# Loads and DMA transposes in strict turns in a fused retention and MLP kernel

## Chip, cores, metric

One core of a Trainium2 chip runs the kernel. The metric is the device time of one execution in microseconds. The profile adds one traced execution: busy times, waits, and the granted clock of the tensor engine. Engines are called PE (matmuls; PEld is its weight load), DVE, ACT, POOL and SP (which only issues DMA here).

## The reference

```python
# q, k, v: (B=4, H=8, S=768, D=64) f32
for t in range(S):                     # retention, per head h, gamma_h = 1 - 2**(-5-h)
    state = gamma * state + outer(k[t], v[t])
    y[t] = q[t] @ state / sqrt(D)
x = y in (B*S, H*D) order              # (3072, 512)
h = x @ w_in                           # (512, 2048)
out = (h * cos(h)) @ w_out             # (2048, 512)
```

## The kernel before

Retention runs in chunks of 128 steps. A "pair" is one chunk of two batch elements; there are 12 pairs, and two pairs make a group of 512 tokens for the MLP. For each pair: load q, k, v; scale q (`conv_q`) and v (`conv_v`) on POOL and cast k (`conv_k`) on ACT, all to bf16; transpose q and k into `qkt`; then on PE `stage_a` (k times q), on DVE its mask (`stage_m`), and on PE `stage_y` (output `xt`, and the state). The MLP's two matmuls (`unit_f`, `unit_o`) fill PE between these. Each engine takes its instructions in the order written.

```python
PRE = 5                                              # slots of load buffers
SLOT = [0, 1, 2, 3, 2, 4, 0, 1, 3, 2, 4, 0]          # pair -> slot
def load(eng, p, names):                             # 256 KB each: one tensor, one batch element
    ...
def conv_k(p, on_act): ...                           # ACT: two casts, one for each batch element
def stage_t(p, b): ...                               # 8 PE transposes and a DVE copy (pairs 0 to 3)
def stage_t_dma(p):                                  # pairs 4 to 11
    for b in range(2):
        nc.sync.dma_start_transpose(out=qkt[n][:, b]..., in_=qk[n][:, b]...)
# ... group 0, pairs 0 to 2 ...
conv_k(3, True); conv_q(3, nc.gpsimd)
load(nc.sync, 4, ("q0", "q1")); load(nc.gpsimd, 4, ("k0", "k1", "v0", "v1"))
conv_v(3, nc.gpsimd)
load(nc.sync, 5, ("q0", "q1", "v0")); load(nc.gpsimd, 5, ("k0", "k1", "v1"))
# ...
stage_t(3, 0); stage_t(3, 1)
# ...
conv_q(4, nc.gpsimd); conv_v(4, nc.gpsimd); conv_k(4, True)
stage_t_dma(4)
load(nc.gpsimd, 6, ("q0", "k0", "q1", "k1", "v0", "v1"))   # two pairs ahead
# ... later: cast and transpose pair p+1, fetch pair p+2 or p+3 ...
```

An output bank of PE (there are seven for all of this) comes free only when ACT and DVE have read it.

Of the kernel before, what the change touches and what calls it, by code (L numbers as in the profile page):

```python
# [10 lines left out]
FP32 = mybir.dt.float32  # L11
BF16 = mybir.dt.bfloat16
# [35 lines left out]
def kernel(  # L48
# [9 lines left out]
    nc = tc.nc  # L58
    B, H, S, D = q.shape
    C = 128  # L60
# [3 lines left out]
    HP = H // 2  # L64
    KIN = DM // 128
    KOUT = DF // 128
    NP = B // 2 * NC
    NG = NP // 2
    PRE = 5
# [11 lines left out]
    def sb(shape, dt, name):  # L81
        return const.tile(shape, dt, name=name)
# [14 lines left out]
    w_out_sb = sb([128, KOUT, DM], BF16, "w_out_sb")  # L97


    qf = [[sb([128, H, D], FP32, f"qf{i}_{b}") for b in range(2)] for i in range(PRE)]  # L100
    kf2 = [sb([128, 2, H, D], FP32, f"kf{i}") for i in range(PRE)]
    kf = [[t[:, b] for b in range(2)] for t in kf2]
    vf = [[sb([128, H, D], FP32, f"vf{i}_{b}") for b in range(2)] for i in range(PRE)]
    ob = [sb([128, DM], FP32, f"ob{i}") for i in range(4)]
    NB = 3
    qk = [sb([128, 2, 2, H, D], BF16, f"qk{i}") for i in range(NB)]
# [11 lines left out]
    gq = sb([128, NC, H], FP32, "gq")  # L118
    gk = sb([128, NC, H], FP32, "gk")
    rel = sb([128, 128], FP32, "rel")  # L120


    SRC = {"q": (qf, q), "k": (kf, k), "v": (vf, v)}
# [3 lines left out]
    def load(eng, p, names):  # L127
        bp, c = divmod(p, NC)
        for n in names:
            t, src = SRC[n[0]]  # L130
            b = int(n[1])
            eng.dma_start(  # L132
                out=t[SLOT[p]][b],
                in_=src[2 * bp + b, :, ds(c * C, C)].rearrange("h t d -> t h d"))

    def load_k(p):
        bp, c = divmod(p, NC)
        nc.gpsimd.dma_start(
            out=kf2[SLOT[p]].rearrange("p b h d -> p (b h) d"),
            in_=k[2 * bp : 2 * bp + 2, :, ds(c * C, C)].rearrange("b h t d -> t (b h) d"))  # L140

    def load_w_in(r):
        nc.gpsimd.dma_start(
# [25 lines left out]
                   allow_small_or_imprecise_dtypes=True)  # L169
    load(nc.gpsimd, 0, ("k1", "q1"))  # L170
    load(nc.gpsimd, 1, ("q1",))
    load_k(1)
    load(nc.gpsimd, 0, ("v0", "v1"))
    nc.vector.memset(zero, 0.0)
    nc.vector.memset(lnsc, math.log(scale))
# [19 lines left out]
    def conv_q(p, eng, bs=(0, 1)):  # L195
        for b in bs:
            eng.tensor_tensor(out=qk[p % NB][:, b, 0], in0=qf[SLOT[p]][b],  # L197
                              in1=bc(gq, p % NC), op=ALU.mult)
            if eng == nc.vector:
                clk.run("dve", 0.69)  # L200

    def conv_v(p, eng, bs=(0, 1)):
        for b in bs:
            eng.tensor_tensor(out=vs[p % NB][:, b], in0=vf[SLOT[p]][b],  # L204
                              in1=bc(gk, p % NC), op=ALU.mult)

    def conv_k(p, on_act):
        for b in range(2):
            if on_act:
                nc.scalar.copy(out=qk[p % NB][:, b, 1], in_=kf[SLOT[p]][b])  # L210
                clk.run("act", 0.6)
            else:
                nc.vector.tensor_copy(out=qk[p % NB][:, b, 1], in_=kf[SLOT[p]][b])
# [12 lines left out]
    def stage_t(p, b, fill=0):  # L226
        n = p % NB
        bank = banks.take()
        tr = bank.bitcast(BF16).rearrange("p (w a t) -> p w a t", w=2, a=HP)
        for w in range(2):  # L230
            for a in range(HP):
                nc.tensor.transpose(tr[:, w, a, :], qk[n][:, b, w, 2 * a : 2 * a + 2, :], ident)  # L232
            if w == 0:
                warm(fill)
        copy_bits(qkt[n][:, b], tr)
        clk.run("pe", 0.45)
        banks.give(bank, clk.run("dve", 0.69, clk.pe + 0.1))

    def stage_t_dma(p):
        n = p % NB  # L240
        for b in range(2):
            nc.sync.dma_start_transpose(
                out=qkt[n][:, b].rearrange("p w a t -> p (w a) t"),
                in_=qk[n][:, b].rearrange("p w h d -> p (w h d)"))
# [7 lines left out]
    def stage_a(p, b):  # L252
        n = p % NB
        bk = [banks.take(), banks.take()]
        ap = [t.rearrange("p (a t) -> p a t", a=HP) for t in bk]
        for a in range(HP):
            for j in range(2):
                po = 64 * j
                nc.tensor.matmul(ap[j][:, a, :], lhsT=kt(n, b, a)[po : po + 64, :],  # L259
                                 rhs=qt(n, b, a)[po : po + 64, :],  # L260
                                 tile_position=(po, 0))
        clk.run("pe", 0.3)
        return b, bk, ap, clk.pe
# [54 lines left out]
    def stage_y(p, copy_st=nc.vector.tensor_copy):  # L318
        for b in range(2):
            half_y(p, b)  # L320
        stage_s(p, copy_st)
# [22 lines left out]
    def pair_f(p, r, parts=(0, 1)):  # L344

        g, hf = divmod(p, 2)
        for f in [4 * r + 2 * i for i in parts]:
            bank = banks.take()
            for e in range(2):
                for i in range(KIN):  # L350
                    nc.tensor.matmul(bank[:, ts(e, 256)], lhsT=w_in_t(i, f + e),  # L351
                                     rhs=xt[g % 2][:, i, ts(hf, 256)],
                                     start=(i == 0 and e == 0), stop=(i == KIN - 1),
                                     skip_group_check=True)
            banks.give(bank, act(bank, gt[g % 2][:, f : f + 2, ts(hf, 256)]))
# [129 lines left out]
    for u in range(12):  # L485
        unit_o(0, u % 4, u // 4)
        if u == 7:
            stage_t(2, 0)
            stage_t(2, 1)
            conv_v(2, nc.vector, (0,))  # L490
        elif u == 9:
            stage_m(2, stage_a(2, 0))
            conv_v(2, nc.vector, (1,))
        elif u == 11:
            stage_m(2, stage_a(2, 1))
    conv_k(3, True)
    conv_q(3, nc.gpsimd)
    load(nc.sync, 4, ("q0", "q1"))
    load(nc.gpsimd, 4, ("k0", "k1", "v0", "v1"))
    conv_v(3, nc.gpsimd)  # L500
    load(nc.sync, 5, ("q0", "q1", "v0"))
    load(nc.gpsimd, 5, ("k0", "k1", "v1"))
    for j in range(4):
        unit_o(0, j, 3)
        if j == 1:
            stage_y(2, nc.scalar.copy)
    pair_f(2, 0)
    stage_t(3, 0)
    stage_t(3, 1)
    pair_f(2, 1)  # L510
    attend(3)
    conv_q(4, nc.gpsimd)
    conv_v(4, nc.gpsimd)
    conv_k(4, True)
    stage_t_dma(4)
    load(nc.gpsimd, 6, ("q0", "k0", "q1", "k1", "v0", "v1"))
    pair_f(2, 2)
    pair_f(2, 3, (0,))
    stage_y(3, nc.scalar.copy)
    pair_f(2, 3, (1,))  # L520
    conv_q(5, nc.gpsimd)
    conv_v(5, nc.gpsimd)
    load(nc.gpsimd, 7, ("q0", "k0", "q1", "k1", "v0", "v1"))
    pair_f(3, 0)
    conv_k(5, True)
    stage_t_dma(5)
    pair_f(3, 1)
    pair_f(3, 2)
    conv_q(6, nc.gpsimd)
    conv_k(6, True)  # L530
    conv_v(6, nc.gpsimd)
    pair_f(3, 3)

    def ahead(p):
        if p < NP:
            conv_q(p, nc.gpsimd)
            conv_k(p, True)
            conv_v(p, nc.gpsimd)

    def fetch(p):  # L540
        load(nc.gpsimd, p, ("q0", "k0", "q1", "k1", "v0", "v1"))

    def later(p):
        stage_y(p)
        n = 8 if p == 4 else p + 3 if p > 5 else NP
        if n < NP:
            fetch(n)

    late = []

    def put_off(when, step):
        late.append((when, step))
# [10 lines left out]
    def o_units(g, a, b):  # L563
        for u in range(a, b):
            unit_o(g, *divmod(u, 4))

    o_units(1, 0, 2)
    attend(4)
    stage_t_dma(6)
    o_units(1, 2, 6)  # L570
    later(4)
    attend(5)
    o_units(1, 6, 10)
    later(5)

    for g in range(2, NG + 1):
        for s in range(16):
            hf, r = divmod(s, 8)
            p = 2 * (g + 1) + hf
            if g == 2 and s % 2 == 0 and s < 12:  # L580
                unit_o(1, *divmod(10 + s // 2, 4))
            if g < NG:
                unit_f(g, s)
            if g > 2:
                if g < NG or s < 12:
                    unit_o(g - 1, *divmod(s, 4))
                elif s == 12:
                    last_o(g - 1, 3)
            while late and late[0][0] <= 16 * g + s:
                late.pop(0)[1]()  # L590
            if p < NP:
                if r == 0:
                    ahead(p + 1)
                elif r == 1:
                    if p + 1 < NP:
                        stage_t_dma(p + 1)
                elif r == 2 and p in (6, 7, 8):
                    todo = [stage_a(p, b) for b in range(2)]
                    stage_m(p, todo[0])
                    put_off(16 * g + s + 1, lambda todo=todo, p=p: stage_m(p, todo[1]))  # L600
                elif r == 6 and p in (6, 7, 11):
                    later(p)
                elif (g, s) == (3, 4):
                    fetch(11)
                if (g, s) in joined:
                    join(joined[g, s], 16 * g + s)


# [28 lines left out]
```

## Time and profile before

| | before |
|---|---|
| time, median (range) | 208.92 us (208.87 to 209.34), 3 runs |
| span of the profiled run | 207.6 us |
| PE busy | 199.5 us (96%) |
| granted clock | 1.0 |
| wait of ACT for k (`kf`) | 9.3 us in 7 waits |
| DMA transpose, issue to landing, min/median/max | 2.7/4.6/13.8 us |

PE is busy nearly all the time and its engine order is the critical chain; the lines are in the prediction. Read a slice line as 40 equal parts of the span, each digit the busy tenths. A wait line reads: engine and line, released by what: us in total, times, longest.

### The profile page before, as it was taken

To read this page: it belongs to the slowest core of one execution; us is meant where nothing else is said; L and a number is where in the kernel's file an instruction comes from. 1 tells how busy PE (TensorE), PEld (TensorE's weight loads), DVE (VectorE), ACT (ScalarE), POOL (GpSimd) and SP (SyncE) were. 2 spreads that over 40 slices of the span, in tenths; PEclk is the share of its full clock that TensorE was granted. 3 is DMA by queue.
4 is the path that set the end of the run, shared out by engine and by line. 5 is a ranking of instruction groups with operands and counts; after the bars stand their busy time and mean duration, and the time that the engine had idled before them with its cause. 6 is when DMAs were issued, how large, how long until landed. Compare 5 with 4: busy or idle time off the path is not lost.

```text
span 207.6 us, 4155 instructions
## 1 busy us (share of the span) xinstructions
PE 199.5 (96%) x1624; PEld 113.5 (55%) x1646; DVE 113.3 (55%) x188; ACT 114.1 (55%) x193; POOL 102.3 (49%) x118
## 2 busy tenths in 40 slices
PE   6889999999999999999999999999999999999993
PEld 1467554558997555546544465544465444444452
DVE  4691984554957454869874466854367244443000
ACT  6767872257996336577753754653554653553120
POOL 8999238399999999999995230000000000000000
PEclk9999999999999999999999999999999999999999
DMA  6999999999999999959799931141101100110222
GB/s 158 351 237 203 215 252 287 336 261 358 258 251 257 264 252 254 255 184 218 242 177 92 252 82 50 55 103 51 51 3 51 51 18 36 51 52 21 80 77 78
DMA packets 36644, 33.83 MB, mean 163 GB/s; under 512 B 26768, under 2 KB 29072, under 8 KB 36624
## 3 DMA queue, kind: packets, MB, share of 16 engines
q0 software_dynamic: 7808, 20.98, 39.4%
q1 hardware_dynamic: 27632, 12.23, 25.4%
q10 hardware_dynamic: 1184, 0.36, 0.7%
q8 instruction: 13, 0.21, 0.4%
q14 instruction: 7, 0.06, 0.1%
HBM read 27.26 MB, written 6.29 MB: 162 GB/s over the span
## 4 chain that ended last, share of the span: by engine, by line
PE 91%; DVE 4%; DMA 2%; issue 1%; DVEq 0%
PE bank L381 38%; PE bank L340 32%; PE bank L351 7%; PE bank L281 3%; PE bank L259 3%; PE bank L286 2%; DMA qf<-in_q_dram 2%; DVE am L268 2%; PE bank L398 2%; PE bank L232 1%; PE st_ps L303 1%; DVE qk L197 1%; DVE qkt L216 1%; PE bank L362 1%; PE bank L369 1%
## 5 line engine op out<-in xcount | busy, mean ns | idle before, releaser
L333 DVE TENSOR_TENSOR gt<-bank,cosb 128x512 bf16<-128x512 f32 x96 | 64.9, 689 | 61.9 <-ACT cosb L329 61.4
L329 ACT ACTIVATE cosb<-bank,halfpi 128x512 bf16<-128x512 f32 x96 | 65.1, 688 | 50.0 <-PE bank L340 44.4
L381 PE MATMUL bank<-w_out_sb,gt 128*128 128x512 bf16 x359 | 88.5, 379 | 0.7 <-issue 0.3
L340 PE MATMUL bank<-xt,w_in 128*128 128x512 bf16 x294 | 74.3, 380 | 0.7 <-issue 0.3
L381 PEld LDWEIGHTS <-gt 128*128 128x128 bf16 x368 | 35.5, 98 | 41.2
L340 PEld LDWEIGHTS <-w_in 128*128 128x128 bf16 x304 | 33.7, 114 | 30.9
L268 DVE TENSOR_TENSOR am<-bank,mask 128x512 bf16<-128x512 f32 x48 | 30.4, 682 | 3.9 <-PE bank L259 3.9
L388 ACT COPY ob<-bank 128x512 f32<-128x512 f32 x23 | 13.4, 586 | 18.4 <-PE bank L381 18.4
L204 POOL TENSOR_TENSOR vs<-vf,gk 128x512 bf16<-128x512 f32 x21 | 21.4, 1045 | 2.9 <-PE st_ps L303 2.9
L132 POOL DMA_DIRECT2D vf<-in_v_dram x23 | 20.3, 885 | 4.8 <-DMA w_out_sb<-in_moe_w_out_dram 4.8
L197 POOL TENSOR_TENSOR qk<-qf,gq 128x512 bf16<-128x512 f32 x18 | 18.5, 1051 | 7.8 <-issue 4.9
L132 POOL DMA_DIRECT2D kf<-in_k_dram x21 | 18.9, 901 | 1.8 <-DMA w_out_sb<-in_moe_w_out_dram 1.6
L210 ACT CAST qk<-kf 128x512 bf16<-128x512 f32 x24 | 13.9, 615 | 9.3 <-DMA kf<-in_k_dram 9.3
L290 ACT CAST xt<-bank 128x512 bf16<-128x512 f32 x24 | 12.9, 589 | 6.7 <-PE bank L286 6.7
L132 POOL DMA_DIRECT2D qf<-in_q_dram x18 | 16.2, 902 | 0.8 <-DMA w_in<-in_moe_w_in_dram 0.8
L351 PE MATMUL bank<-xt,w_in 128*128 128x256 bf16 x128 | 14.7, 273 | 0.0
L351 PEld LDWEIGHTS <-w_in 128*128 128x128 bf16 x128 | 13.8, 114 | 0.4
L286 PE MATMUL bank<-am,vs 128*64 128x128 bf16 x192 | 11.6, 220 | 0.0
L281 PEld LDWEIGHTS <-stb 128*64 128x64 bf16 x160 | 8.7, 109 | 4.3 <-issue 3.8
L281 PE MATMUL bank<-qkt,stb 128*64 128x128 bf16 x160 | 10.7, 222 | 0.3 <-DVE am L268 0.3
L286 PEld LDWEIGHTS <-vs 128*64 128x64 bf16 x192 | 9.9, 110 | 0.5 <-issue 0.4
L315 DVE CAST stb<-st_ps 64x512 bf16<-64x512 f32 x12 | 8.2, 685 | 2.7 <-PE st_ps L303 2.6
(46 smaller groups left out, 86.8 us busy)
## 6 DMA issues: line engine op xcount, KB each, us to landing
vf<-in_v_dram POOLq DMA_DIRECT2D x23, 256.0 KB, 5.8
out_dram<-ob SPq DMA_DIRECT2D x23, 256.0 KB, 2.0
kf<-in_k_dram POOLq DMA_DIRECT2D x21, 256.0 KB, 5.7
qf<-in_q_dram POOLq DMA_DIRECT2D x18, 256.0 KB, 5.3
w_out_sb<-in_moe_w_out_dram POOLq DMA_DIRECT2D x4, 512.0 KB, 12.5
qf<-in_q_dram SPq DMA_DIRECT2D x6, 256.0 KB, 8.1
w_in<-in_moe_w_in_dram POOLq DMA_DIRECT2D x3, 512.0 KB, 8.1
kf<-in_k_dram POOLq DMA_DIRECT2D x1, 512.0 KB, 5.4
```

Source lines behind the costliest of these rows:

```text
L132: eng.dma_start(out=t[SLOT[p]][b], in_=src[2 * bp + b, :, ds(c * C, C)].rearrange("h t d -> t h d"))
L197: eng.tensor_tensor(out=qk[p % NB][:, b, 0], in0=qf[SLOT[p]][b], in1=bc(gq, p % NC), op=ALU.mult)
L204: eng.tensor_tensor(out=vs[p % NB][:, b], in0=vf[SLOT[p]][b], in1=bc(gk, p % NC), op=ALU.mult)
L210: nc.scalar.copy(out=qk[p % NB][:, b, 1], in_=kf[SLOT[p]][b])
L268: nc.vector.tensor_tensor(out=am[p % 2][b][j], in0=ap[j], in1=mask.unsqueeze(1).to_broadcast([128, HP, 128]), op=ALU.mult)
L281: nc.tensor.matmul(yp[ts(j, 64), a, :], lhsT=stb[p % 2][:, b, a, ts(j, 64)], rhs=qt(n, b, a), start=True, stop=False, skip_group_check=True)
L286: nc.tensor.matmul(yp[ts(j, 64), a, :], lhsT=vs[n][:, b, 2 * a + j, :], rhs=am[p % 2][b][j][:, a, :], start=(c == 0), stop=True, skip_grou ...
L329: nc.scalar.activation(out=cb, in_=bank, func=AF.Sin, bias=halfpi)
L333: nc.vector.tensor_tensor(out=out, in0=bank, in1=cb, op=ALU.mult)
L340: nc.tensor.matmul(bank, lhsT=w_in_t(i, f), rhs=xt[g % 2][:, i, :], start=(i == 0), stop=(i == KIN - 1))
L351: nc.tensor.matmul(bank[:, ts(e, 256)], lhsT=w_in_t(i, f + e), rhs=xt[g % 2][:, i, ts(hf, 256)], start=(i == 0 and e == 0), stop=(i == KIN ...
L381: nc.tensor.matmul(bank, lhsT=gt[g % 2][:, f, ts(j, 128)], rhs=w_out_sb[:, f, :], start=(f == 0), stop=(f == KOUT - 1))
```

## The change

The intent, as its description and code tell it: no DMA transpose is to share the DMA engines with loads. From pair 3 on a turn is: cast on POOL, transpose, wait for the transpose, only then load the next pair, with q, k and v in one 512 KB transfer each. POOL is held by a tiny copy (`gate`) that reads the output of the first of a pair's two transposes; the second may still run beside the new loads. Pair 3 moves from PE transposes to DMA transposes, and most k casts move to other places in ACT's order: those of pairs 3, 4 and 8 to 11 earlier, that of pair 6 later.

```diff
-    qf = [[sb([128, H, D], FP32, f"qf{i}_{b}") for b in range(2)] for i in range(PRE)]
...
+    both = {n: [sb([128, 2, H, D], FP32, f"{n}f{i}") for i in range(PRE)] for n in "qkv"}
+    gate = sb([128, 2], BF16, "gate")
+    def load_both(p, names):                       # 512 KB each: both batch elements
...
+    def turn(p):
+        conv_q(p, nc.gpsimd)
+        stage_t_dma(p)
+        conv_v(p, nc.gpsimd)
+        if p + 1 < NP:
+            nc.gpsimd.tensor_copy(out=gate, in_=qkt[p % NB][:, 0, 1, HP - 1, 126:])
+            load_both(p + 1, "kqv")                # one pair ahead
...
-    stage_t(3, 0)
-    stage_t(3, 1)
...
+    k_at = {(2, 0): 7, (2, 6): 8, (2, 12): 9, (3, 4): 10, (3, 12): 11}   # casts, (group, unit)
+    t_at = {(2, 1): 7, (2, 8): 8, (2, 15): 9, (3, 6): 10, (3, 13): 11}   # turns
```

Before, the casts of pairs 7 to 11 stood at (2,0), (2,8), (3,0), (3,8), (4,0).

More of the change, by code (lines that the diff above doesn't have):

```diff
@@ L97 @@
     w_out_sb = sb([128, KOUT, DM], BF16, "w_out_sb")
-    qf = [[sb([128, H, D], FP32, f"qf{i}_{b}") for b in range(2)] for i in range(PRE)]
-    kf2 = [sb([128, 2, H, D], FP32, f"kf{i}") for i in range(PRE)]
-    kf = [[t[:, b] for b in range(2)] for t in kf2]
-    vf = [[sb([128, H, D], FP32, f"vf{i}_{b}") for b in range(2)] for i in range(PRE)]
+    both = {n: [sb([128, 2, H, D], FP32, f"{n}f{i}") for i in range(PRE)] for n in "qkv"}
+    qf, kf, vf = [[[t[:, b] for b in range(2)] for t in both[n]] for n in "qkv"]
     ob = [sb([128, DM], FP32, f"ob{i}") for i in range(4)]
@@ L134, in load @@
                 in_=src[2 * bp + b, :, ds(c * C, C)].rearrange("h t d -> t h d"))
-    def load_k(p):
+    def load_both(p, names):
         bp, c = divmod(p, NC)
-        nc.gpsimd.dma_start(
-            out=kf2[SLOT[p]].rearrange("p b h d -> p (b h) d"),
-            in_=k[2 * bp : 2 * bp + 2, :, ds(c * C, C)].rearrange("b h t d -> t (b h) d"))
+        for n in names:
+            nc.gpsimd.dma_start(
+                out=both[n][SLOT[p]].rearrange("p b h d -> p (b h) d"),
+                in_=SRC[n][1][2 * bp : 2 * bp + 2, :, ds(c * C, C)].rearrange(
+                    "b h t d -> t (b h) d"))
     def load_w_in(r):
@@ L171 @@
     load(nc.gpsimd, 1, ("q1",))
-    load_k(1)
+    load_both(1, "k")
     load(nc.gpsimd, 0, ("v0", "v1"))
@@ L493 @@
             conv_v(2, nc.vector, (1,))
+            conv_k(3, True)
         elif u == 11:
             stage_m(2, stage_a(2, 1))
-    conv_k(3, True)
-    conv_q(3, nc.gpsimd)
-    load(nc.sync, 4, ("q0", "q1"))
-    load(nc.gpsimd, 4, ("k0", "k1", "v0", "v1"))
-    conv_v(3, nc.gpsimd)
-    load(nc.sync, 5, ("q0", "q1", "v0"))
-    load(nc.gpsimd, 5, ("k0", "k1", "v1"))
+    def turn(p):
[5 more added lines that the diff above has]
+            load_both(p + 1, "kqv")
+    turn(3)
     for j in range(4):
@@ L507 @@
     pair_f(2, 0)
-    stage_t(3, 0)
-    stage_t(3, 1)
+    conv_k(4, True)
     pair_f(2, 1)
     attend(3)
-    conv_q(4, nc.gpsimd)
-    conv_v(4, nc.gpsimd)
-    conv_k(4, True)
-    stage_t_dma(4)
-    load(nc.gpsimd, 6, ("q0", "k0", "q1", "k1", "v0", "v1"))
+    turn(4)
     pair_f(2, 2)
@@ L520 @@
     pair_f(2, 3, (1,))
-    conv_q(5, nc.gpsimd)
-    conv_v(5, nc.gpsimd)
-    load(nc.gpsimd, 7, ("q0", "k0", "q1", "k1", "v0", "v1"))
     pair_f(3, 0)
     conv_k(5, True)
-    stage_t_dma(5)
     pair_f(3, 1)
+    turn(5)
     pair_f(3, 2)
-    conv_q(6, nc.gpsimd)
-    conv_k(6, True)
-    conv_v(6, nc.gpsimd)
     pair_f(3, 3)
-    def ahead(p):
-        if p < NP:
-            conv_q(p, nc.gpsimd)
-            conv_k(p, True)
-            conv_v(p, nc.gpsimd)
-    def fetch(p):
-        load(nc.gpsimd, p, ("q0", "k0", "q1", "k1", "v0", "v1"))
-    def later(p):
-        stage_y(p)
-        n = 8 if p == 4 else p + 3 if p > 5 else NP
-        if n < NP:
-            fetch(n)
     late = []
@@ L568 @@
     attend(4)
-    stage_t_dma(6)
-    o_units(1, 2, 6)
-    later(4)
+    o_units(1, 2, 4)
+    conv_k(6, True)
+    o_units(1, 4, 6)
+    turn(6)
+    stage_y(4)
     attend(5)
     o_units(1, 6, 10)
-    later(5)
+    stage_y(5)
+    k_at = {(2, 0): 7, (2, 6): 8, (2, 12): 9, (3, 4): 10, (3, 12): 11}
+    t_at = {(2, 1): 7, (2, 8): 8, (2, 15): 9, (3, 6): 10, (3, 13): 11}
+    a_at = {(2, 2): 6, (2, 10): 7, (3, 2): 8}
+    y_at = {(2, 6): 6, (2, 14): 7, (4, 14): 11}
     for g in range(2, NG + 1):
         for s in range(16):
-            hf, r = divmod(s, 8)
-            p = 2 * (g + 1) + hf
             if g == 2 and s % 2 == 0 and s < 12:
@@ L588 @@
                     last_o(g - 1, 3)
-            while late and late[0][0] <= 16 * g + s:
+            now = 16 * g + s
+            while late and late[0][0] <= now:
                 late.pop(0)[1]()
-            if p < NP:
-                if r == 0:
-                    ahead(p + 1)
-                elif r == 1:
-                    if p + 1 < NP:
-                        stage_t_dma(p + 1)
-                elif r == 2 and p in (6, 7, 8):
-                    todo = [stage_a(p, b) for b in range(2)]
-                    stage_m(p, todo[0])
-                    put_off(16 * g + s + 1, lambda todo=todo, p=p: stage_m(p, todo[1]))
-                elif r == 6 and p in (6, 7, 11):
-                    later(p)
-                elif (g, s) == (3, 4):
-                    fetch(11)
-                if (g, s) in joined:
-                    join(joined[g, s], 16 * g + s)
+            at = (g, s)
+            if at in k_at:
+                conv_k(k_at[at], True)
+            if at in t_at:
+                turn(t_at[at])
+            if at in a_at:
+                p = a_at[at]
+                todo = [stage_a(p, b) for b in range(2)]
+                stage_m(p, todo[0])
+                put_off(now + 1, lambda todo=todo, p=p: stage_m(p, todo[1]))
+            if at in y_at:
+                stage_y(y_at[at])
+            if at in joined:
+                join(joined[at], now)
 _INS = ['q', 'k', 'v', 'moe_w_in', 'moe_w_out']
```

## The prediction

> **What bounds the kernel now.** I read the page first: busy times, slices, chain; then the waits of the tensor engine, the chain in order of time, and the timelines of POOL and ACT. From the page:
>
> ```profile
> PE 199.5 (96%) x1624; PEld 113.5 (55%) x1646; DVE 113.3 (55%) x188; ACT 114.1 (55%) x193; POOL 102.3 (49%) x118
> ...
> PE   6889999999999999999999999999999999999993
> ...
> POOL 8999238399999999999995230000000000000000
> ...
> DMA  6999999999999999959799931141101100110222
> ...
> PE 91%; DVE 4%; DMA 2%; issue 1%; DVEq 0%
> ```
>
> PE is busy in every slice but the first three and the last. POOL is full to about 110 us and then does nothing; DMA is full to about 118 us. So the changed parts (loads, transposes) work in the first 60% of the span and are hidden: PE is what ends late. The waits of PE and the chain in order of time confirm it:
>
> ```profile
> PE bank L415 <- DVE gt L174: 1.2, 1, 1.2
> PE bank L259 <- DVE qkt L216: 1.1, 2, 0.6
> ```
>
> ```profile
> 49.39 0.89 PE bank L232 x16
> ...
> 52.03 0.55 PE bank L259 x16
> ...
> 77.91 1.73 PE bank L340 x8
> ...
> 93.90 3.58 PE bank L340 x16
> 97.47 0.18 PE bank L281 x2
> ...
> 98.91 1.67 PE bank L340 x7
> ```
>
> The longest two waits of PE are at the start (the warm-up and the first transposes). From 16 us to 204 us the chain is PE after PE. Eight matmuls of 512 columns take 1.73 us, 216 ns each, so nothing is to be had by feeding PE better: time falls only if PE work goes, and rises only if something new makes PE wait.
>
> **What the Trainium skill says.** "TensorE: Matmul & The Clock Gate", section "Wait — 56ns, not 53.3ns?", gives 215.7 ns for 512 columns at full clock; the trace agrees (216 ns, granted clock 1.0 in all slices). "DMA: Bandwidth & Descriptors", section "Issuing engines are not separate DMA queues", says that transfers from all issuers share the same 16 DMA engines and interleave; the trace agrees: one transpose took 2.7 us to land when no load ran (136 us) and 13.8 us in the middle of loads (104 us). The same page, section "Anatomy of one DMA — SWDGE (gpsimd) path", puts a POOL transfer at 2.0 us fixed plus bytes over 436 GB/s, 2.6 us for 256 KB; the trace disagrees: 3.8 us at the best in this stretch, issue of 0.88 us included, so I use the trace. The same page, section "Rules for kernel authors", says that a transpose beside ordinary DMAs needs nothing, so the gate is for speed, not for correctness; no run shows it yet.
>
> **The change, part by part.** Removed from PE: the 16 transposes of pair 3 (in the chain above at 49.39), 0.89 us on the path. Their two copies by DVE (681 ns each) were hidden. Pair 3 now takes two DMA transposes, as do pairs 4 to 11 in both kernels. That is all that PE gains: 208.92 - 0.89 = 208.0 us if nothing waits. No other PE work changes in amount; only places of the k casts in ACT's order and of the loads in POOL's.
>
> Loads: 8 pairs times 6 transfers of 256 KB become 8 times 3 of 512 KB. POOL pays 0.88 us for each of the first kind and 1.15 us for the one 512 KB load of before (4.19 us), so 3.45 us in place of 5.3 us a pair. POOL ran the old cycle without a pause, 9.3 us a pair:
>
> ```profile
> 69.49 2.05 POOL L197 TENSOR_TENSOR qk<-qf,gq 128x512 bf16<-128x512 f32 x2
> 71.49 2.04 POOL L204 TENSOR_TENSOR vs<-vf,gk 128x512 bf16<-128x512 f32 x2
> 73.48 0.93 POOL L132 DMA_DIRECT2D qf<-in_q_dram  x1
> 74.40 0.88 POOL L132 DMA_DIRECT2D kf<-in_k_dram  x1
> ```
>
> There a load was issued two pairs ahead, so its landing time was hidden. In the new order POOL does conv_q, conv_v, then the gate (which reads the first transpose's output, so it waits for its landing), then issues the next pair's k, q, v; and the next conv_q needs that q. Now landing is on POOL's cycle. One turn, gate to gate: issue k 1.15; q from issue start to landing, estimated at 4.0 (256 KB loads at 64 to 74 us took 3.8 to 4.7) plus 0.3 longer issue plus 0.3 to 0.8 for twice the data at the 390 GB/s which the busiest moments show: 4.5 to 5.1; conv_q and conv_v 2.05 + 2.04; gate and signals 0.3. The first transpose runs beside conv_v: it starts 1.1 after q, lands 3.1 later (the one at 134.5 us, without loads), q + 4.2, about when conv_v ends, q + 4.1. Sum 10.0 to 10.7, I take 10.3 us. So POOL's work falls, but the cycle grows from 9.3 to about 10.3 us, and no load is ahead of it.
>
> What of it meets PE? The second transpose lands about 1.3 after the gate; k lands about 4.8 after it. Gates: pair 3's inputs land near 40 us as before; the gate of pair 4 cannot come before its k cast, which ACT reaches at 50.2 (behind the two cosines of pair_f(2,0)), so near 54.2. Then 64.5, 74.8, 85.1, 95.4 for pairs 5 to 8. PE's wants, from the chain less 0.89: stage_a of pair 4 at 65.5, 5 at 70.9, 6 at 80.5, 7 at 92.4, 8 at 104, 9 at 119.8, 10 at 128.6. The transposes meet all of them with margin. The k casts don't. They sit in ACT's strict order ahead of work that PE needs:
>
> ```profile
> 91.38 1.12 ACT L210 CAST qk<-kf 128x512 bf16<-128x512 f32 x2
> 92.41 0.69 ACT L329 ACTIVATE cosb<-bank,halfpi 128x512 bf16<-128x512 f32 x1
> ...
> 98.10 1.06 ACT L290 CAST xt<-bank 128x512 bf16<-128x512 f32 x2
> ```
>
> Before, no k cast after 60 us waited for its load. Now the cast of pair 9 is moved ahead from (3,0) to (2,12), where ACT arrives at about 95.5, and its k lands at 95.4 + 4.8 = 100.2. Behind it in ACT stand two cosines (1.3) and the two casts of xt of pair 7 (1.07), after its own 1.12: xt is ready 3.5 after k lands, at 103.7. PE wants it for unit_f(3,0), in the chain inside the piece at 98.91, less 0.89: 98.7. That is a wait of 5.0 us. Pairs 7 (k at 79.3, PE has banks until it lands at 78.6) and 8 (89.6 against some 88.6) cost up to 1 us, inside the 5.0 and not on top, since loads don't wait for PE. Pairs 10 and 11 have 12 and 15 us more of PE work between them and recover. Sum: 208.92 - 0.89 + 5.0 = 213.0 us by this reckoning.
>
> **The rivals.** First, turns are quick enough. With a cycle of 9.4 us pair 9's k lands at about 96 and PE waits 0.7 us at most; the time is 208 to 209. For it: transposes free of loads take 2.7 to 3.1 us, not the median 4.6; whoever placed the casts 8 to 9 us apart reckoned with such a cycle. Against it: conv_q and conv_v alone take 4.1 us and q can hardly land within 5 us of the gate. Second, the cycle is slower: output stores of 256 KB come into some turns, the second transpose overlaps the new loads, 512 KB of short rows is not moved at the best rate. Each 0.5 us in the cycle counts four times at pair 9: with 10.8 us the time is 215. Third, less DMA traffic in PE's way: excluded, since PE runs at 216 ns for a matmul both while DMA is full (77.91, above) and after. Fourth, a wait for pair 3: PE wants its transposes at 51.1, they are issued near 41 to 43, and even 5.6 us (the first transposes under loads) would do. PE's slack here is 3 us; I give it little weight. A gain of over 2% would take 4.2 us of PE time; 0.89 is all there is.
>
> **Range and chances.** The sum says 213.0, the first rival 208.3. The error of the sum is mostly the cycle, plus or minus 0.4 times four and 1 us for ACT's place, and it can only go down to 208.0. I put two thirds on the sum and one third on the rival: 211.5, with 208.0 to 214.8 for 8 in 10. Slower by 2% begins at 213.1: 0.32. Faster by 2%: 0.01. The same: 0.67.
>
> **What would show it.** If right: no piece of L232 near 50 us in the chain, and 16 PE and 2 DVE instructions fewer of that line; POOL no longer full in its slices but with a wait for a qkt transpose and one for q in each turn; transposes landing in about 3 us; ACT waiting for kf between 77 and 101 us, longest for pair 9, some 4 to 5 us; PE idle just before unit_f(3,0), waiting for ACT's cast of xt. POOL's turns end near 125 us instead of 122. If instead ACT waits for kf less than 1 us, the cycle was under 9.5 us and the first rival holds. If PE waits for qkt from a DMA, I was wrong about which product of a turn comes last. If the 216 ns of a matmul change, the third rival was excluded wrongly.

## The result, and the profile after

The changed kernel took 230.69 us, median of 6 runs (228.66 to 231.39); the kernel before 208.89 us in the same rounds. The ratio is 1.102 (95% interval 1.098 to 1.107): slower by 10%. A ratio here and below is the mean time of one kernel's fast runs over the mean of the other's of the same rounds, so not quite the ratio of the medians. Executions over 1.5% slower than the fastest of the same kernel are left out of the means. The profiled run is the quickest of the six: span 225.8 us, granted clock 0.977.

From the page of the changed kernel, busy times, slices and chain:

```profile
PE 203.6 (90%) x1608; PEld 113.8 (50%) x1630; DVE 111.9 (50%) x186; ACT 114.2 (51%) x193; POOL 94.0 (42%) x107
...
PE   7889999999999690999639999999999999999994
...
POOL 8997255856767273947667671500000000000000
PEclk9999999999999998599988999999999999999999
...
PE 68%; DMA 17%; POOL 5%; DVE 4%; issue 3%; ACT 2%; POOLq 0%; ACTq 0%; DVEq 0%
```

PE now has two deep holes (near 87 us and near 113 us), in and after which its clock falls, and a shallow one near 76 us, after which it does not. PE has 16 instructions fewer than before and yet 4 us more of busy time. POOL is no longer full: it waits. The chain, nearly all PE before, now runs through DMA and POOL for over a fifth of the span. The waits say for what:

```profile
POOL qk L198 <- DMA qf<-in_q_dram: 33.7, 9, 5.3
ACT qk L211 <- DMA kf<-in_k_dram: 29.0, 13, 6.6
...
PE bank L341 <- ACT ob L389: 6.5, 1, 6.5
...
PE bank L341 <- ACT xt L291: 5.3, 1, 5.3
...
PE bank L382 <- ACT xt L291: 2.0, 1, 2.0
```

PE waits 13.8 us for ACT, ACT 29 us for k's loads, POOL 34 us for q's. One turn in POOL's timeline (start, us, what; in brackets the idle time before it and who ended it), from the gate of pair 6 to that of pair 7:

```profile
82.72 0.19 POOL L503 COPY gate<-qkt 128x2 bf16<-128x2 bf16 x1 [1.09 <-DMA qkt<-qk]
83.29 1.19 POOL L138 DMA_DIRECT2D kf<-in_k_dram  x1 [0.39 <-issue]
84.48 1.15 POOL L138 DMA_DIRECT2D qf<-in_q_dram  x1
85.62 1.16 POOL L138 DMA_DIRECT2D vf<-in_v_dram  x1
90.29 2.04 POOL L198 TENSOR_TENSOR qk<-qf,gq 128x512 bf16<-128x512 f32 x2 [3.51 <-DMA qf<-in_q_dram]
92.29 2.04 POOL L205 TENSOR_TENSOR vs<-vf,gk 128x512 bf16<-128x512 f32 x2
94.28 0.18 POOL L503 COPY gate<-qkt 128x2 bf16<-128x2 bf16 x1
```

This turn took 11.6 us. The eight gates stand at 44.7, 57.0, 68.3, 82.7, 94.3, 107.6, 118.9 and 130.9 us: 12.3 us a turn in the mean, 11.2 to 14.5. Before, POOL's cycle was 9.3 us. From gate to conv_q, in which POOL issues and then waits for q, it is 7.2 to 7.6 us in six of the eight turns and 9.3 in two. In that stretch the DMA engines stand still first. Windows of half a microsecond behind the gate of pair 5 (the last two figures are DMA share and GB/s):

```profile
68.50:69.00 0.50, 0.50 (x4) 0.23 (x3) 0.50 (x2) 0.00 (x0) 0.20 (x1) 1.00 1.19 209
69.00:69.50 0.50, 0.50 (x4) 0.26 (x3) 0.50 (x2) 0.33 (x1) 0.50 (x1) 1.00 0.00 0
69.50:70.00 0.50, 0.50 (x4) 0.20 (x2) 0.50 (x2) 0.26 (x1) 0.50 (x2) 1.00 0.00 0
70.00:70.50 0.50, 0.50 (x4) 0.20 (x2) 0.45 (x1) 0.00 (x0) 0.50 (x1) 1.00 0.08 8
```

The first load was issued at 68.80; the DMA engines, until then busy with earlier transfers, fall idle at 69.0 and move next to nothing until 70.5 us. On ACT the k casts stand where PE needs ACT:

```profile
88.62 1.14 ACT L211 CAST qk<-kf 128x512 bf16<-128x512 f32 x2 [6.58 <-DMA kf<-in_k_dram]
...
113.16 1.14 ACT L211 CAST qk<-kf 128x512 bf16<-128x512 f32 x2 [5.20 <-DMA kf<-in_k_dram]
114.20 1.26 ACT L330 ACTIVATE cosb<-bank,halfpi 128x512 bf16<-128x512 f32 x2
115.35 1.07 ACT L291 CAST xt<-bank 128x512 bf16<-128x512 f32 x2
```

The first is the cast of pair 7; while ACT waited for its k, PE ran out of banks. The second is pair 9's; behind it stand two cosines and the xt casts that unit_f(3,0) needs. PE's timeline shows its two long waits, and windows of the unit_f matmuls (after the window its length, then PE's busy time in these matmuls, and PEclk as the third figure from the end) show what follows:

```profile
90.87 1.86 PE L341 MATMUL bank<-xt,w_in 128*128 128x512 bf16 x4 [6.46 <-ACT ob L389]
...
116.47 1.86 PE L341 MATMUL bank<-xt,w_in 128*128 128x512 bf16 x4 [5.27 <-ACT xt L291]
```

```profile
90.80:97.10 6.30, 4.61 (x12) 1.48 (x11) 0.59 0.61 140
...
116.40:120.00 3.60, 2.03 (x5) 0.68 (x5) 0.53 0.65 148
```

After each long wait PE ran at a granted clock of 0.59 and 0.53 for 6.3 and 3.6 us. Four matmuls took 1.86 us there against 0.86 us in the rest of the chain.

### The profile page after: what moved, and what is told of

Read it like the earlier page. It is cut to its first block, busy times and chain, and to the rows that moved or that the text cites. A ratio compares the mean times of both kernels' runs of the same rounds, so it can differ in the third digit from the quotient of the medians.

```text
span 225.8 us, 4084 instructions
## 1 busy us (share of the span) xinstructions
PE 203.6 (90%) x1608; PEld 113.8 (50%) x1630; DVE 111.9 (50%) x186; ACT 114.2 (51%) x193; POOL 94.0 (42%) x107
## 4 chain that ended last, share of the span: by engine, by line
PE 68%; DMA 17%; POOL 5%; DVE 4%; issue 3%; ACT 2%; POOLq 0%; ACTq 0%; DVEq 0%
PE bank L382 30%; PE bank L341 28%; DMA qf<-in_q_dram 8%; DMA kf<-in_k_dram 5%; DMA vf<-in_v_dram 3%; DMA qkt<-qk 2%; DVE am L269 2%; PE bank L399 2%; PE bank L260 2%; POOL vs L205 2%; PE bank L282 1%; POOL kf L138 1%; PE bank L287 1%; POOL qk L198 1%; ACT cosb L330 1%
## 5 line engine op out<-in xcount | busy, mean ns | idle before, releaser
L382 PE MATMUL bank<-w_out_sb,gt 128*128 128x512 bf16 x359 | 90.3, 385 | 2.8 <-ACT xt L291 2.0
L341 PE MATMUL bank<-xt,w_in 128*128 128x512 bf16 x294 | 76.9, 390 | 12.4 <-ACT ob L389 6.5
L382 PEld LDWEIGHTS <-gt 128*128 128x128 bf16 x368 | 35.9, 99 | 44.7 <-issue 4.5
L341 PEld LDWEIGHTS <-w_in 128*128 128x128 bf16 x304 | 34.4, 116 | 44.6 <-issue 15.3
L198 POOL TENSOR_TENSOR qk<-qf,gq 128x512 bf16<-128x512 f32 x18 | 18.5, 1045 | 34.1 <-DMA qf<-in_q_dram 33.7
L205 POOL TENSOR_TENSOR vs<-vf,gk 128x512 bf16<-128x512 f32 x21 | 21.9, 1066 | 0.7 <-DMA vf<-in_v_dram 0.7
L352 PEld LDWEIGHTS <-w_in 128*128 128x128 bf16 x128 | 13.8, 114 | 0.7 <-issue 0.3
L138 POOL DMA_DIRECT2D kf<-in_k_dram x9 | 10.7, 1189 | 2.2 <-issue 1.5
L282 PE MATMUL bank<-qkt,stb 128*64 128x128 bf16 x160 | 10.7, 222 | 0.3 <-DVE am L269 0.3
L260 PE MATMUL bank<-qkt 64*128 64x128 bf16 x192 | 8.2, 218 | 1.3 <-DVE qkt L217 1.1
L138 POOL DMA_DIRECT2D vf<-in_v_dram x8 | 9.2, 1152 | 0.0
L138 POOL DMA_DIRECT2D qf<-in_q_dram x8 | 9.2, 1152 | 0.0
## 6 DMA issues: line engine op xcount, KB each, us to landing
w_out_sb<-in_moe_w_out_dram POOLq DMA_DIRECT2D x4, 512.0 KB, 12.3
```

The source lines that it names most:

```text
L138: nc.gpsimd.dma_start(out=both[n][SLOT[p]].rearrange("p b h d -> p (b h) d"), in_=SRC[n][1][2 * bp : 2 * bp + 2, :, ds(c * C, C)].rearrang ...
L198: eng.tensor_tensor(out=qk[p % NB][:, b, 0], in0=qf[SLOT[p]][b], in1=bc(gq, p % NC), op=ALU.mult)
L205: eng.tensor_tensor(out=vs[p % NB][:, b], in0=vf[SLOT[p]][b], in1=bc(gk, p % NC), op=ALU.mult)
L282: nc.tensor.matmul(yp[ts(j, 64), a, :], lhsT=stb[p % 2][:, b, a, ts(j, 64)], rhs=qt(n, b, a), start=True, stop=False, skip_group_check=True)
L341: nc.tensor.matmul(bank, lhsT=w_in_t(i, f), rhs=xt[g % 2][:, i, :], start=(i == 0), stop=(i == KIN - 1))
L352: nc.tensor.matmul(bank[:, ts(e, 256)], lhsT=w_in_t(i, f + e), rhs=xt[g % 2][:, i, ts(hf, 256)], start=(i == 0 and e == 0), stop=(i == KIN ...
```

## The experiments

All kernels gave correct results. "Before" in the same rounds was 208.9 to 209.0 us throughout.

**Loads two pairs ahead, gate kept.**

```diff
+        if p == 3:
+            load_both(4, "kqv")
-        if p + 1 < NP:
+        if p + 2 < NP:
             nc.gpsimd.tensor_copy(out=gate, ...)
-            load_both(p + 1, "kqv")
+            load_both(p + 2, "kqv")
```

> The changed kernel with one thing moved: the loads of a turn are those of the pair after the next (pair 4's loads go out before the first gate); gate, three transfers of 512 KB and the places of the casts stay. Theory (a load that is only one pair ahead puts its landing, 5 to 7.5 us, on the turn's cycle, and the k casts then hold up ACT): each load has a whole turn to land, ACT's waits for kf fall from 29 us to under 10 us, POOL's waits for q from 34 us to under 8 us, the mean clock is 1.0 again, and the time is 208 to 210 us. Rival (gate or large transfers themselves slow the turn): POOL still waits and the time stays above 220 us.

Measured 216.75 us (4 runs, 215.53 to 218.28), ratio 1.038. ACT's wait for k fell to 9.6 us and POOL's for q to 0.8 us, as expected, but the clock did not come back to 1.0 (0.992) and the time is a miss by 7 us. The wait went elsewhere. From this run's waits, and the transposes' landing (min/median/max):

```profile
POOL gate L505 <- DMA qkt<-qk: 21.3, 6, 5.2
```

```profile
DMA to landing us min/median/max: 2.7/5.3/9.3
```

POOL issues the loads for two pairs later and goes straight on to the next conv_q, so the next transposes run among these loads after all, land in 5.3 us in place of the changed kernel's 2.8 us, and the gate waits for them. POOL's turn stays at 10.7 to 12.6 us (gates at 62.4, 73.4, 86.0, 96.9). What look-ahead bought is that k and q are there when wanted, 14 of the 22 us; what is left is mostly PE's waits for transposes (4.9 us in the trace) and a slow clock behind one of them.

**Without the gate.** One line taken out of the changed kernel, the gate copy.

> The changed kernel without the gate copy, so that POOL issues the next pair's loads as soon as it has done conv_v. Theory: the gate costs 3.6 us of waits and eight times some 0.6 us of its own and restart, about 0.8 us a turn of 12, so pair 7's and 9's k come 3 to 5 us earlier and the time is 223 to 228 us. Rival (holding transposes and loads apart is what costs): the time falls to under 214 us.

Measured 225.20 us (4 runs, 223.92 to 226.57), ratio 1.078: as the theory had it. The gate itself is a quarter of the loss. Without it POOL stands before conv_q just the same, 3 to 5 us in every turn (the profile puts six of these waits down to "issue"; q lands in 5.3 to 7.4 us from its issue in this run), since the next pair's loads still stand behind this pair's conv_v.

**Six transfers of 256 KB in place of three of 512 KB.**

```diff
-            load_both(p + 1, "kqv")
+            load(nc.gpsimd, p + 1, ("k0", "k1", "q0", "q1", "v0", "v1"))
```

> The changed kernel with each turn's three transfers of 512 KB issued as six of 256 KB (k, k, q, q, v, v). Theory (the order of the turn costs, not the size of a transfer): POOL's issue grows by 1.8 us a turn, the first q lands earlier; the two about cancel, 227 to 233 us. Rival (a 512 KB transfer must land whole before the cast of either batch element can start, and that is the cost): at or below 218 us.

Measured 221.07 us (5 runs, 218.94 to 226.08), ratio 1.058. Both expectations were wrong: the size of a transfer does cost, some 10 us of the 22, though not all. The two DMA tables (size, median us from issue to landing) show why; the changed kernel:

```profile
kf<-in_k_dram POOLq DMA_DIRECT2D x9, 512.0 KB, 5.3
qf<-in_q_dram POOLq DMA_DIRECT2D x8, 512.0 KB, 5.8
```

and with six transfers:

```profile
qf<-in_q_dram POOLq DMA_DIRECT2D x22, 256.0 KB, 4.8
kf<-in_k_dram POOLq DMA_DIRECT2D x21, 256.0 KB, 4.2
```

By these medians a half lands about 1 us earlier, and its cast can start while the other half comes. POOL's wait for q falls from 33.7 to 11.4 us, against 1.8 us more of issue a turn; the gate of pair 9 comes at 111.4 in place of 118.9 us.

**The k casts later in ACT's order.** Pair 7 from (2,0) to (2,5), 8 from (2,6) to (2,13), 9 from (2,12) to (3,5), 10 from (3,4) to (3,10), 11 from (3,12) to (3,15), the turns one unit behind each; pair 6 behind `stage_y(5)`.

> The changed kernel with the k casts of pairs 6 to 11, and so their turns, at later places in ACT's order (pair 7 from (2,0) to (2,5), 8 from (2,6) to (2,13), 9 from (2,12) to (3,5), 10 from (3,4) to (3,10), 11 from (3,12) to (3,15), 6 behind stage_y(5)). Theory (casts that wait in ACT's order hold up cosines and xt casts that PE needs): ACT's waits for kf fall below 15 us, PE's waits on ACT fall from 13.8 us to a few, and what remains is PE's waiting for transposes, 3 to 6 us: 211 to 216 us. Rival (the length of the turn sets the end whatever the place of the casts): 226 to 233 us.

Measured 217.66 us (4 runs, 215.13 to 219.65), ratio 1.032. By the median that is the theory's direction, 2 us more than its range; the two fast runs, 215.13 and 216.01 us, lie in it or at its edge. ACT still waits 16.6 us for k (expected: below 15), but PE waits for ACT only once. PE's longest waits in the trace are now 1.9 us (for an xt cast) and 1.2 us (for a transpose), and that run's clock is 1.0; two of the timed runs, at 0.98, took 3 to 4 us longer and don't enter the ratio. So most of the loss, 13 of 22 us by the medians and 15 by the fast runs, needs a k cast that stands too early in ACT's order for its load; the turns themselves are as long as in the changed kernel (gates from 44.9 to 134.0 us, 12.7 us a turn).

**The kernel before with large transfers.** Pairs 6 to 11 loaded with three transfers of 512 KB at the old places.

> The kernel before with the loads of pairs 6 to 11 as three transfers of 512 KB in the old places, two pairs or more ahead, nothing else. Theory (large transfers land later, which hurts only where a cast waits for them): the landing stays hidden, POOL's cycle falls from 9.3 to about 7.5 us, PE doesn't notice: 208.5 to 209.5 us. Rival (three large transfers cost by themselves): over 213 us.

Measured 209.78 us (4 runs, 208.95 to 211.52), ratio 1.004 (0.9998 to 1.0085): no cost that can be told from noise. So, as far as this run and the six-transfer run go, large transfers cost only where the loads are one pair ahead. Here the transposes took longer to land (median 6.4, longest 12.7 us), and in the profiled run PE waited 0.9 us for one.

**The kernel before with pair 3 transposed by DMA.**

```diff
     conv_q(3, nc.gpsimd)
+    stage_t_dma(3)
     load(nc.sync, 4, ("q0", "q1"))
...
-    stage_t(3, 0)
-    stage_t(3, 1)
```

> The kernel before with pair 3 transposed by two DMA transposes in place of 16 PE transposes. Theory: PE loses 0.89 us of work, 208.0 to 208.3 us, if the transposes, which lie among loads here, land before 51.1 us; if they land later, PE waits and the time is 209 to 213 us. Rival (this part of the change is what costs): over 215 us.

Measured 246.92 us median of 6, ratio 1.155 by its two fast runs: 239.53 to 248.01 in five runs and 530.62 in the profiled one. That is the rival's range (but see below: it is not what costs in the changed kernel). In that profiled run matmuls of 512 columns took 0.83 us from the start to the end, at a granted clock shown as 1.0; this I can't explain, and it was not seen again.

> The kernel of e6 once more for a trace, since its profiled run had PE slow from the start, unlike its five timed runs of 240 to 248 us. Theory: the transposes of pair 3 or the loads of pairs 4 and 5 behind them in SP's queue land much later than PE wants them: a wait of PE of some 10 us or more near 51 us or near 65 us, and a granted clock below 1 after it. Rival: PE is slow from the start again, and the cause is not in this kernel's order.

Measured 243.1 us (a single run), like the timed runs, span 241.3 us, PE not slow from the start. PE's waits and clock slices, and the transposes' landing:

```profile
PEclk9999999999967755976997999999999999999999
```

```profile
PE bank L259 <- DMA qkt<-qk: 26.7, 6, 7.6
```

```profile
DMA to landing us min/median/max: 2.7/10.2/26.6
```

Pair 3's own transposes landed in 3.4 to 4.3 us, in time. But SP issues in order, and behind them its loads of pairs 4 and 5, which it issued between about 34 and 44 us in the kernel before, went out between 44 and 53 us here. The transposes of pairs 4 to 6, issued from 58 us on, took 10 to 27 us each, and PE's waits for DMA transposes, 26.7 us in six, begin at 65 us, not near 51 us. That the late loads are the cause is argued from this order; what the record shows is that pair 3's DMA transposes alone are not: with the loads of pairs 4 and 5 on POOL behind a gate the loss is gone ("Only the first turn", 209.08 us). So a small shift throws the kernel before off its balance, and holding transposes and loads apart has a reason. Why transposes fall so far behind is open; that they go in packets under 512 B beside loads in larger ones is a guess.

**Two pairs ahead, no gate.** The first experiment without the gate line.

> The first experiment (loads two pairs ahead) with the gate taken out too. In that one POOL waited 21 us at the gate, since the loads issued ahead slow the transposes that the gate waits for. Theory (look-ahead and gate are at odds, and either a short look-ahead or a gate puts transfers on POOL's cycle): 207.9 to 210 us, POOL's waits for transposes and q both near zero. Rival (the early places of the casts in ACT's order or the large transfers cost even with look-ahead): 213 us or more.

Inconclusive: 211.75 to 223.08 us over 6 runs, too scattered. In the profiled run (216.66 us) the transposes took 7.9 us to land in the median and up to 20.2 us, and POOL waited 9.9 us for q. The theory's range was reached by no run. Five of the six lie in the rival's, but the waits of this trace (3.7 us of PE for transposes, none for ACT of note) speak for the collision of loads and transposes rather than for the rival's reasons.

**The kernel before with gates.** A gate copy in front of the loads of pairs 6 to 11, waiting for the transposes of the pair two earlier.

> The kernel before with a gate copy in front of the loads of pairs 6 to 11 (each waits for the transposes of the pair two earlier), six transfers of 256 KB, casts in their old places, pair 3 on PE. Theory (the gate lengthens POOL's cycle from 9.3 to about 11 us, but the loads are two pairs ahead and the casts late enough, so PE hardly waits): 208.9 to 212 us. Rival (holding transposes and loads apart is itself what cost the changed kernel its 22 us): over 220 us.

Measured 210.92 us (4 runs, 210.36 to 211.38), ratio 1.009 (1.008 to 1.011). The gate alone, with loads two pairs ahead and the casts at their old places, costs 2 us, not 22.

**Only the first turn.** The kernel before with pair 3 transposed by DMA ahead of a gate, and the loads of pairs 4 and 5 (three of 512 KB each) behind it.

> The kernel before with only the first turn of the change: pair 3 transposed by DMA with no load beside it, the gate, then the loads of pairs 4 and 5 as three transfers of 512 KB each; everything from pair 6 on as in the kernel before. Theory (a DMA transpose without loads beside it lands in some 3 us, in time for PE at 51 us, and 16 PE transposes go): 207.9 to 208.5 us, the only version that beats both kernels. Rival (the early part of the changed kernel costs as well): 211 us or more.

Measured 209.08 us (6 runs, 208.36 to 210.25), ratio 1.001 (0.999 to 1.004). Between theory and rival, and no gain that can be told: about half of the removed 0.89 us shows in the two best runs and nothing of it in the others. It was the candidate for a version that beats both, and it doesn't beat the kernel before.

**Late casts and six transfers.** The two edits shown above in one kernel.

> Two experiments in one: the changed kernel with late casts and with six transfers of 256 KB a turn. Theory (PE's waits follow from the length of the turn and the place of the casts, nothing else): the turn falls to about 11 us as with six transfers, the k casts no longer stand before it, so the transposes of pairs 6, 7, 8 and 10 land within 1 us of PE's want: 208.5 to 212.5 us. Rival (a further cost remains in DMA transposes that follow loads so closely): 215 us or more, as with late casts alone.

Measured 211.61 us (4 runs, 210.83 to 212.31), ratio 1.012: the time as the theory had it, but not by its way. The turn did not fall to 11 us: gates from 44.9 to 129.7 us make 12.1 us a turn, near the changed kernel's 12.3. What is gone is the waiting: from the cast of pair 6 on no k cast waits for its load, and PE waits 0.2 us for ACT in place of 13.8. With both edits the turns' order and gate remain and the kernel comes within 2.7 us of the one before. The clock is 1.0; PE's one long wait is 1.2 us for the transposes of pair 6. So a turn of 12 us is affordable when nothing that PE needs stands behind its loads.

**q first.** The changed kernel with loads in the order q, k, v.

> The changed kernel with each turn's loads in the order q, k, v in place of k, q, v. Theory (the landing of q, which POOL waits for before conv_q, is on the turn; k has only ACT behind it): the turn falls from 12.3 by about 1.2 us to 11.0 to 11.3 us; k lands 1 us later after its gate, but at pair 7 the gate is 3.5 us earlier and at pair 9 6 us: PE's waits fall by some 6 us and its slow clock with them, 219 to 225 us. Rival (k's landing sets the turn through the transpose): 229 us or more.

Measured 226.62 us (4 runs, 224.34 to 228.64), ratio 1.080: a gain of 4 us, half of what I expected, between both expectations. Through the gate of pair 9 a turn took 11.8 us, not 11.1. POOL's wait for q fell from 33.7 to 18.3 us, but a wait of 10.0 us for v appeared before conv_v. Not q alone is on the turn but the three loads together. And k, now second, came later for the cast of pair 4, which ACT reaches early: ACT waited 3.0 us for it, PE 3.0 us behind ACT (until 55.6 us), and PE's clock was 0.50 from there to 60 us, a loss that the changed kernel does not have.

## Why the prediction was wrong

The path was right in the main, its length was not. PE bound; no PE transposes of pair 3, PE down by 16 instructions; POOL no longer full and waiting for q; ACT waiting for kf; PE held just before unit_f(3,0) by the xt casts behind pair 9's cast: all of this is in the trace as the prediction had it, and late casts (13 us less by the medians, 15 by the fast runs) shows that the casts' place in ACT's order carries most of it. Even the arithmetic "xt is ready 3.5 after k lands" held: the cast starts at 113.16, PE goes on at 116.47, 3.3 us later. Not as predicted: the longest wait of ACT and of PE is at pair 7, not at pair 9; the gate waits for a transpose in three turns, not in each; POOL's turns end at 144 us, not near 125.

The step that failed is the term "One turn, gate to gate ... I take 10.3 us", and with it the arrival of pair 9's k, put at 100.2 us and measured at 113.1. The 12.9 us come out in three parts.

- The first turn: pair 4's gate was put at 54.2 by ACT's place; measured at 57.2 at its end. POOL was waiting for q (conv_q at 52.28) and v (conv_v at 55.04), not for ACT: 3.0 us.
- Four turns from there to the gate of pair 8, which ends at 107.8: 12.65 us each, not 10.3: 9.4 us.
- k's landing, 5.3 us after the gate's end and not 4.8: 0.5 us.

Inside the turn, q's landing from its issue was put at 4.5 to 5.1 us and measured at 5.4 to 5.8 in five turns, 6.2 in one and 7.5 in two. The base of 4.0 for 256 KB held: in the six-transfer run k's halves, first in each turn, took 3.7 to 4.6 us. Too small was what came on top: 512 KB of k, first in the queue, took 4.9 to 6.0 us, and q, issued right behind it, 0.3 to 0.8 us more in six turns and 1.5 and 2.2 in the two slow ones. The sum had no term for k's data ahead of q's. In the last experiment the two change places: q, first, took 5.5 us in the median and k 6.2. Then there were 0.1 to 0.6 us from the gate's start to the first issue, and up to 1.7 us in which the gate waited for a transpose; I had 0.3 for all signals. Why two of the turns (loads of pairs 6 and 11, the same buffer) took 7.5 us for q is open.

The clock was missed. "TensorE: Matmul & The Clock Gate", section "Part 1: The HAM clock gate (the "warmup" mystery)", says that an idle window of some 3.4 us sets PE back to half its clock. The changed kernel's trace fits: granted clock 0.59 and 0.53 after waits of 6.5 and 5.3 us, and 1.0 throughout in the late-cast run, whose waits were under 2 us. Other traces show that 3.4 us of waiting is not needed: the clock was 0.50 after a wait of 2.3 us (loads two pairs ahead, 86.7 to 90.0 us) and of 3.0 us (q first, 55.6 to 60 us), and 1.0 after one of 2.5 us (six transfers, at 109 us). PE's busy time is 203.6 against 199.5 - 0.89 = 198.6 us: 5.0 us more, which I put down to the clock (a mean of 0.977 over 225.8 us makes 5.2). With 13.8 us of waits and 0.89 saved that makes 207.6 + 17.9 = 225.5 of the 225.8 us of span. The prediction's way of counting gives nearly the same: unit_f(3,0) was wanted at 98.7 and started at 116.47, 17.8 us late, so 207.6 - 0.89 + 17.8 = 224.5, and the rest is mostly the slow clock that came after it. The longer wait, at pair 7, lies inside these 17.8, as the prediction had it for a short one: it put k of pair 7 at 79.3 us and a cost of up to 1 us, and ACT's cast began at 88.6 and PE waited 6.5 us.

Of the rivals, the second (a slower cycle) is what happened. It had q's delay for a partial reason, "512 KB of short rows is not moved at the best rate", and was worked out for only 0.5 us more a turn, so that 215 us was its figure; the turns took 2.35 us more. The first rival, turns quick enough, got a third of the weight, in part on the ground that someone had placed the casts so. That was no evidence. The third and fourth rivals were rightly set aside: matmuls stayed at 216 ns outside the slow clock, and pair 3's transposes (issued from 40.9, landed in 2.8 and 3.3 us) met PE in time. Two slips in the prediction changed nothing: k of pairs 7 and 8 should stand at 79.6 and 89.9 by its own 4.8 us, and POOL was not full all the way to 110 us (slices of 2, 3 and 3 tenths between 21 and 42 us).

Which part of the change costs what, by the experiments: the parts don't add up, since each takes away lateness at the same few places. Out of some 22 us, by the means of the fast runs, taking the early casts away gives back 15, look-ahead 14, small transfers 10, the gate 5, q first 4 to 5; small transfers and late casts together 19. The order "one pair ahead, behind the transposes" with casts placed for a shorter turn is the cause; the gate by itself on the kernel before costs 2 us and large transfers nothing that can be told. Not run: the early casts alone in the kernel before.

## What to carry to other kernels

When a transfer loses its look-ahead, add its whole time from issue to landing to the cycle, and take it at the size and at the place in the queue that it will have. An engine that works in strict order must not take on a step that waits for a transfer until the latest place that still serves; here PE's waits of 2.3 to 6.5 us mostly cost again as a slow clock. Keep transposes and loads apart only with loads far enough ahead to pay for it.

## What the Trainium skill lacked or had wrong

- "DMA: Bandwidth & Descriptors", section "Anatomy of one DMA — SWDGE (gpsimd) path": 2.0 us plus bytes over 436 GB/s makes 3.2 us for 512 KB (an estimate from the page's formula). Measured from the start of issue to landing: 5.3 us in the median for the first load of a turn, with no other load in flight, 1.2 us of it POOL's issuing; in the windows shown some 1.7 us pass from the start of issue to the first bytes.
- The same page, section "Rules for kernel authors", says that a transpose next to ordinary DMAs needs nothing. As to results that holds in all runs here. As to time it lacks a warning: 2.7 us alone, up to 26.6 us among loads (pair 3 by DMA, second run).
- "TensorE: Matmul & The Clock Gate", section "Part 1: The HAM clock gate (the "warmup" mystery)": the idle window of some 3.4 us is not a safe limit for a wait. The clock was 0.50 after waits of 2.3 and 3.0 us, and 1.0 after one of 2.5 us.
- No page that I read follows a late load through an engine that works in strict order (here ACT) to PE's banks; here 2 us more a turn became 18 us of span that way.
